# Block 6 of a Strassen GEGLU kernel: another order of its pairs, and other places for a normalization and two weight sums

## The chip, the cores and the metric

The kernel runs on 1 core of one Trainium2 chip. The metric is device time in microseconds (us). The kernel before takes 296.37 us, the median of 3 runs (296.33 to 296.41). TensorE (PE) multiplies, VectorE (DVE), ScalarE (ACT) and GpSimd (POOL) do the rest, and SyncE (SP) issues most DMAs.

## What is computed

An efficient attention (softmax of q over the head's dimension, softmax of k over the sequence, then q times the small matrix k^T v) feeds a gated feed-forward block:

```python
q_s = softmax(q, axis=-1); k_s = softmax(k, axis=2)
kv = np.einsum('bhsd,bhse->bhde', k_s, v)
attn = np.einsum('bhsd,bhde->bhse', q_s, kv)          # 8 batches, 8 heads, 576 x 64
x = attn.transpose(0, 2, 1, 3).reshape(4608, 512)
g = x @ w_gate                                         # 512 x 1536
val = x @ w_val
out = (gelu(g) * val) @ w_out                          # 1536 x 512
```

## The kernel before, in words

The rows of x are worked off in nine blocks of 512: blocks 0 to 7 are the first 512 rows of each batch, and block 8 (B in the code) collects the 64 rows that remain of each of the eight batches. The order is 0 to 6, then 8, then 7. For a block the kernel computes twelve tiles of 128 columns of g and val, applies the gate, keeps the result h as f16 in `ht`, and multiplies it by w_out.

Blocks 0 and 1 compute g and val directly. From block 2 on, much of this is done by a Strassen-Winograd scheme with seven products instead of eight, both for the first multiplication and for the second (`out_strassen`, from block 1 on).

*First multiplication.* Two tiles of columns, k and k + 3, make a pair (`pair_step`, line 662). A pair takes four steps, written "k.i": step 1 does products 1 and 5, step 2 products 6 and 3, step 3 products 7 and 2, step 4 product 4. Each product is four matmuls of 128x256 (`product_gv`, line 626). Between them ACT and DVE carry partial sums: `snap` copies a PSUM tile to SBUF (snq), `add` adds PSUM and snapshot into `cc`, `final` and `upper` apply the gate and write `ht`. The result `cc` of every second pair is kept in the memory of a free buffer (named eq in the profile), the other in a tile of its own. Columns that are not in a pair are done by `half` (line 652): "8g" or "8v" is the gate or value half of tile 8 as four matmuls of 128x512.

The order is a string for each block (lines 641 to 648), worked off by `go_on`. A word "k.i" is a step of a pair, "8g" a half, and any other word calls what the plan holds under that name. FOUR (blocks 2 and 3) has four pairs and four whole tiles, FIVE (blocks 4 and 5) five pairs and two whole tiles (8 and 11), SIX6 (block 6) and SIX (blocks 8 and 7) six pairs. SIX6 knows a step 0, which does product 1 of a pair alone ahead of step 1; its first six steps run at the end of block 5 (lines 860 and 861), before the copy that empties tile psa.

*Sums of the inputs.* The pairs need four differences of parts of x, in `xs`: `sum_x` (line 620) computes them on GpSimd, `sum_x6` (line 613), for block 6 alone, two on GpSimd and two on DVE. They need sums of weights as well: `sum_w1` (line 604) computes those of a late pair, spread over blocks 1 to 5. The sums for pair 8 are needed only by blocks that do pair 8.

*Second multiplication.* `out_strassen` (line 770) does seven products of 12 matmuls each into the PSUM tiles psa, psb and psc, in the order 1, 2, 5, 6, 3, 7, 4 (in blocks 2 to 5 product 7 stands ahead of the last two matmuls of product 3). DVE or ACT takes snapshots (`sn`), and DVE adds them into `yo`, which is stored. The sums of h that products 5, 6 and 3 need are made by `sum_h` (line 576, tiles sh, s and ht) on DVE and GpSimd. The last step of the last pair lies within product 1: in blocks 2 to 5 after three of the six parts of it (`four`, line 804), else after four.

*Other work.* A plan, `at(b, kind, i, functions)`, hangs work on points of a block, and `ride` calls it there: PR points are the words of the order string and a few names, NS points lie within the second multiplication (NS 1 behind the snapshot of psc, NS 2 behind the second snapshot of psa). So the softmax of batch n + 1 is spread over block n: in blocks 2 to 6 its normalizing sums are words "a" and "n" (`norm_pair`, line 233, a reduction of 1280 columns each on DVE), its multiplications words "a", "m" and "p" on GpSimd, and its transposing DMA word "t". `norm_rem0` (line 272) normalizes 64 left-over rows of q of batch 0: a reduction and a reciprocal on DVE, a multiplication on GpSimd, at word "u0" of block 5. Its result goes into a transposing DMA in block 6.

The program is written out in order by hand: every engine runs its instructions in the order in which the code issues them, and a wait holds up all that stands behind it on that engine. PSUM has eight banks, handed out in turn by `big` and `let_go`.

Of the kernel before, what the change touches and what calls it, by code (L numbers as in the profile page):

```python
# [12 lines left out]
ALU = mybir.AluOpType  # L13
# [5 lines left out]
def kernel(  # L19
# [10 lines left out]
    nc = tc.nc  # L30

    B, H, S, D = q.shape
# [4 lines left out]
    NFI = F // P  # L37
# [11 lines left out]
    NO = NFI // 2  # L49
# [43 lines left out]
    def let_go(t):  # L93
        ring.append(held.pop(id(t))[1])
# [19 lines left out]
    xs = const.tile([P, 4, 2, 256], f16)  # L114
# [290 lines left out]
    def get_xt(b):  # L405
        if (b, "xt") not in st:
            st[(b, "xt")] = att.tile([P, HP, MAIN], f16, name="xt", tag="xt")
        return st[(b, "xt")]
# [201 lines left out]
                       3: (a21, a11, a21, ALU.subtract), 4: (t[2], a12, t[1], ALU.subtract)}[i]  # L610
        (nc.gpsimd if eng == "pool" else nc.vector).tensor_tensor(out=o, in0=a, in1=b, op=op)

    def sum_x6():
        xt = get_x(6)
        b11, b12, b21, b22 = (xt[:, c:c + 2, r:r + 256] for c in (0, 2) for r in (0, 256))
        for eng, o, a, b in ((nc.gpsimd, 0, b12, b11), (nc.vector, 1, b22, xs[:, 0]), (nc.vector, 2, b22, b12),
                             (nc.gpsimd, 3, b21, xs[:, 1])):
            eng.tensor_tensor(out=xs[:, o], in0=a, in1=b, op=ALU.subtract)

    def sum_x(xt, xs=xs):  # L620
        b11, b12, b21, b22 = (xt[:, c:c + 2, r:r + 256] for c in (0, 2) for r in (0, 256))
        t = [xs[:, i] for i in range(4)]
        for o, a, b in ((t[0], b12, b11), (t[1], b22, t[0]), (t[2], b22, b12), (t[3], b21, t[1])):
            nc.gpsimd.tensor_tensor(out=o, in0=a, in1=b, op=ALU.subtract)

    def product_gv(i, ps, xt, k, first):
        lo, hi = slice(k * P, (k + 1) * P), slice((k + NO // 2) * P, (k + NO // 2 + 1) * P)
        xs = xs_b[xt is st.get((B - 1, "xt"))]
        for t, w, nm in ((0, wv_sb, "v"), (1, wg_sb, "g")):
# [11 lines left out]
    FOUR = ("a 7g l 7v n 0.1 6.1 0.2 6.2 0.3 6.3 m p 10g 0.4 6.4 1.1 t 10v 1.2 8g 1.3 s0 8v u0 1.4 2.1"  # L641
            " 11g 2.2 11v 2.3 s1")
    FIVE = ("a 8g l 8v n m 0.1 6.1 0.2 6.2 0.3 6.3 0.4 1.1 p 6.4 7.1 t 1.2 7.2 1.3 s0 7.3 2.1 1.4 u0 11g 2.2"
            " y 7.4 11v 2.3 s1")
    SIX6 = ("0.0 6.0 0.1 6.1 a 0.2 6.2 n 0.3 6.3 m 0.4 1.1 6.4 p 7.1 t 1.2 7.2 1.3 s0 7.3 u0 1.4 2.1 7.4 8.1 2.2"
            " 8.2 2.3 8.3 s1 2.4")
    SIX = ("0.1 6.1 0.2 6.2 0.3 6.3 0.4 1.1 6.4 7.1 s0 1.2 7.2 1.3 u0 7.3 1.4 2.1 7.4 8.1 2.2"
           " 8.2 2.3 s1 8.3 2.4")
    steps = {b: (SIX if b >= B - 1 else SIX6 if b == 6 else FIVE if b > 3 else FOUR).split() for b in range(2, B + 1)}
    live, begun = {}, {}  # L650

    def half(b, xt, c, nm):
        t = big([P, 512], f32, "ps" + nm)
# [8 lines left out]
    def pair_step(b, xt, k, i):  # L662
        def final(ps, fi):
            gl = ffn.tile([P, 256], f32, name="glq", tag="gl")
            nc.scalar.activation(out=gl, in_=ps[:, 1], func=ACTF.Gelu)  # L665
            nc.vector.scalar_tensor_tensor(out=ht[:, fi, 0:256], in0=ps[:, 0], scalar=_H_SCALE,  # L666
                                           in1=gl, op0=ALU.mult, op1=ALU.mult)
            let_go(ps)

        def snap(ps, dve=False):  # L670
            sn = ffn.tile([P, 2, 256], f32, name="snq", tag="snq")
            if dve:
                nc.vector.tensor_scalar(out=sn, in0=ps, scalar1=_H_SCALE, scalar2=None, op0=ALU.mult)
            else:
                nc.scalar.activation(out=sn, in_=ps, func=ACTF.Copy, scale=_H_SCALE)  # L675
            return sn

        def add(o, ps, sn):
            nc.vector.scalar_tensor_tensor(out=o, in0=ps, scalar=_H_SCALE, in1=sn,  # L679
                                           op0=ALU.mult, op1=ALU.add)  # L680

        def upper(cc):
            nc.scalar.activation(out=cc[:, :, 1], in_=cc[:, :, 1], func=ACTF.Gelu,  # L683
                                 scale=1.0 / _H_SCALE)
            (nc.vector if k == NFI - NO // 2 - 1 else nc.gpsimd).tensor_tensor(  # L685
                out=ht[:, k:k + NO // 2 + 1:NO // 2, 256:512], in0=cc[:, :, 0], in1=cc[:, :, 1],
                op=ALU.mult)

        if i == 1 and k in begun:
            cc, pa, pb = begun.pop(k)  # L690
        elif i < 2:
            live["odd"] = odd = not live.get("odd", True)
            cc = cc_b[b > 2] if odd else ffn.tile([P, 2, 2, 256], f32, name="cc", tag="cc", bufs=1)
            pa = big([P, 2, 256], f32, "pga", True)
            product_gv(1, pa, xt, k, True)
            pb = big([P, 2, 256], f32, "pgb", True, True)
            nc.scalar.copy(out=pb, in_=pa)  # L697
            if i == 0:
                begun[k] = (cc, pa, pb)
                return  # L700
        if i == 1:
            pc = big([P, 2, 256], f32, "pgc", True)
            product_gv(5, pc, xt, k, True)
            live[k] = [cc, pa, pb, pc, snap(pc, b >= B - 1 or b > 3 and k % NO == 1)]
            return
        cc, pa, pb, pc, s5 = live[k]
        if i == 2:
            product_gv(6, pa, xt, k, False)
            s2 = snap(pa)
            product_gv(3, pc, xt, k, False)  # L710
            add(cc[:, 0], pc, s2)
            let_go(pc)
        elif i == 3:
            product_gv(7, pa, xt, k, False)
            add(cc[:, 1], pa, s5)
            product_gv(2, pb, xt, k, False)
            final(pb, k)
            if k == NFI - NO // 2 - 1 or 3 < b < B - 1 and (k < 2 or k == NO or b == 6):
                live["late"] = lambda: upper(cc)
            elif 3 < b < B - 1 and k == NO + 1:  # L720
                live["y"] = lambda: upper(cc)
            else:
                upper(cc)
        else:
            product_gv(4, pa, xt, k, False)
            if steps[b] and steps[b][0].endswith(".1"):
                live["late"] = lambda: final(pa, k + NO // 2)
            else:
                final(pa, k + NO // 2)

    def go_on(b, xt, upto=None):
        while steps[b] and upto != 0:
            x = steps[b].pop(0)
            late = live.pop("late", None) if "." in x else None
            if "." in x:
                k, i = x.split(".")
                pair_step(b, xt, int(k), int(i))
                upto = upto - 1 if upto else None
            elif x[-1] in "gv" and x[:-1].isdigit():
                half(b, xt, int(x[:-1]), x[-1])  # L740
            elif x == "y":
                live.pop("y")()
            else:
                ride(b, PR, x)
            if late:
                late()
# [17 lines left out]
    def get_x(b):  # L764
        return get_xt(b) if b < B else xtr
# [4 lines left out]
    def out_strassen(b, last):  # L770
        yo = [yop.tile([P, 2, C], f32, name="yo", tag="yo") for _ in range(2)]
        c = (slice(0, 256), slice(256, 512))
# [28 lines left out]

        js = (0, 1, 2, 3, 4, 5) if b < 2 else (0, 3, 1, 4, 2, 5)
        get("a")
        four = 1 < b < B - 2
        cut = 3 if four else 4
        product(1, ps["a"], True, js=js[:cut])
        if four:
# [2 lines left out]
        ride(b, NS, 0)  # L810
        if b < 4:
            ride(b, PR, "u1")
        if b >= B - 2:
            pair_step(b, get_x(b), NFI - NO // 2 - 1, 4)
        get("b")
        product(1, ps["a"], False, js=js[4:])
        if b > 1:
            s1 = snap("a", True)
# [5 lines left out]
        if b < 2:  # L824
            s1 = snap("a")
# [31 lines left out]
        if b == B:  # L857
            go_on(B - 1, get_x(B - 1), 1)
        product(4, ps["a"], False, js=js)
        if b == 5:  # L860
            go_on(6, get_x(6), 6)
        nc.scalar.activation(out=yo[1][:, :, c[0]], in_=tiles_["a"][0], func=ACTF.Copy,
                             scale=1.0 / _H_SCALE)
        let_go(tiles_["a"][0])
# [98 lines left out]
    FI, NS, PR = range(3)  # L963
    plan = {}

    def at(b, kind, i, *fns):
        plan.setdefault((b, kind, i), []).extend(fns)

    L = lambda f, *a: (lambda: f(*a))
# [39 lines left out]
    for b in range(2, B):  # L1009
        n = b + 1  # L1010
# [9 lines left out]
            at(b, PR, "e", L(exp, "q", n + 1), L(exp, "k", n + 1))  # L1020
    at(4, PR, "l", load_rem0)
    at(4, PR, "e", exp_rem0)
    at(5, PR, "u0", norm_rem0)
    at(6, PR, "t", L(unit_trem, 0))
    for b in range(2, B - 1):
        n = b + 1
        at(b, NS, 4, L(unit_x4, n, ("act", "dve"), 0 if n == B - 1 else None))
        at(b, NS, 0, L(unit_kv4, n, True))
        if b < 6:
            at(b, NS, 4, L(preload, ACTF.Gelu))  # L1030
        at(b, NS, 4, sum_x6 if n == 6 else L(lambda n: sum_x(get_x(n)), n if n < B - 1 else B))
    at(B, NS, 2, L(lambda: sum_x(get_x(B - 1), xs_b[1])))
    for b in range(2, B + 1):
        for j in range(NO // 2 - 1):
# [9 lines left out]
                    at(b, PR, "u0", L(sum_h, j, NO, (2,)), L(sum_h, j, NO, (4,), "pool"))  # L1044
    for b, kind, i, dk, x in ((1, FI, 6, 0, 1), (1, FI, 6, 0, 2), (1, FI, 6, 0, 4), (1, FI, 9, 0, 3),
                              (2, NS, 2, 1, 1), (2, NS, 2, 1, 2), (3, NS, 2, 1, 4), (3, NS, 2, 1, 3),
                              (4, NS, 2, 2, 1), (4, NS, 2, 2, 2), (5, NS, 2, 2, 4), (5, NS, 2, 2, 3)):
        at(b, kind, i, L(sum_w1, x, NO + dk, "pool" if b < 2 else "dve"))


    def ride(b, kind, i):
        for fn in plan.get((b, kind, i), []):
            fn()

    for b in order:
        xt = get_xt(b) if b < B else xtr
# [60 lines left out]
```

## Time and profile before

| what | us |
|---|---|
| median of 3 runs | 296.37 |
| the profiled execution | 296.37 |
| its span, first to last instruction | 294.6 |
| PE busy | 282.2 (96%) |
| DVE busy | 231.7 (79%) |
| ACT busy | 199.4 (68%) |
| GpSimd busy | 193.6 (66%) |

The mean granted clock of TensorE is 0.998. 1.77 us of the profiled execution lie outside the span. PE is busy almost throughout, but not quite: the chain of work that ended last is by 87% on PE, by 5% on DVE and by 2% each on GpSimd and ACT.

```profile
PE 87%; DVE 5%; POOL 2%; ACT 2%; issue 2%; ACTq 1%; POOLq 0%
```

In such a chain a share of DVE or GpSimd is a stretch in which PE was held up by that engine. A row of the timeline reads: start, duration, engine, line, operation, output and inputs with shapes, number of instructions merged, and in brackets the idle time of the engine before it and what ended that. Durations of matmuls overlap: the distance of their starts is what they cost.

### The profile page before, as it was taken

The numbers are of one execution on the slowest core, as the hardware profiler recorded it, in microseconds if no ns is written. First come the engines' busy times: TensorE is split into PE (matmuls) and PEld (weight loads), VectorE is DVE, ScalarE is ACT, GpSimd is POOL, SyncE is SP. The second block draws the span as 40 slices with busy tenths as digits, with TensorE's granted clock in tenths as the row PEclk, the third lists the DMA queues.
The fourth block names the chain that finished last, engine by engine and source line by source line (L and its number), as shares of the span: only waits on it lengthen the run. The fifth ranks groups of instructions, "written<-read, shape, count | busy, mean of one in ns | idle before, by whom it ended". The sixth has DMA issues, their size and how long they took to land.

```text
span 294.6 us, 6525 instructions
## 1 busy us (share of the span) xinstructions
PE 282.2 (96%) x2509; PEld 208.4 (71%) x2509; DVE 231.7 (79%) x435; ACT 199.4 (68%) x336; POOL 193.6 (66%) x178
## 2 busy tenths in 40 slices
PE   3999999999999999999999999989799999999994
PEld 1544445446777787778787878777687888888883
DVE  2955889868996789678988898888969579938992
ACT  3763367776687589768967896769675477537650
POOL 1557747995487679857986789766782466293640
PEclk9999999999999999999999999999999999999999
DMA  6999999998069605980598049901150110033003
GB/s 219 373 382 389 401 391 391 333 334 232 3 214 381 121 2 183 384 149 2 163 375 196 2 153 371 193 2 71 73 98 2 75 72 2 1 72 73 2 0 144
DMA packets 54623, 51.73 MB, mean 176 GB/s; under 512 B 18496, under 2 KB 50496, under 8 KB 54592
## 3 DMA queue, kind: packets, MB, share of 16 engines
q1 hardware_dynamic: 52864, 49.49, 53.5%
q10 hardware_dynamic: 1728, 1.84, 1.9%
q8 instruction: 19, 0.31, 0.4%
q14 instruction: 12, 0.10, 0.1%
HBM read 37.75 MB, written 9.44 MB: 160 GB/s over the span
## 4 chain that ended last, share of the span: by engine, by line
PE 87%; DVE 5%; POOL 2%; ACT 2%; issue 2%; ACTq 1%; POOLq 0%
PE pga L636 19%; PE psa L760 13%; PE psg L471 10%; PE psv L471 10%; PE pgc L636 10%; PE psc L760 7%; PE pgb L636 4%; PE psb L760 4%; PE psy L539 4%; PE pswarm L463 2%; PE pskv L347 1%; POOL ht L685 1%; DVE yo L798 1%; ACT L466 1%; POOL s L586 1%
## 5 line engine op out<-in xcount | busy, mean ns | idle before, releaser
L636 PEld LDWEIGHTS <-wgv_sb 128*128 128x128 f16 x576 | 55.7, 98 | 12.9 <-DVE cc L679 1.8
L471 PEld LDWEIGHTS <-wgv_sb 128*128 128x128 f16 x288 | 27.9, 98 | 29.1 <-issue 0.7
L760 PEld LDWEIGHTS <-ht 128*128 128x128 f16 x384 | 36.5, 98 | 9.2 <-issue 2.5
L248 POOL TENSOR_TENSOR eq<-eq,rrq 128x640 f16<-128x640 f16 (+1 forms) x27 | 34.8, 1304 | 12.1 <-DVE rrq L240 8.8
L685 POOL TENSOR_TENSOR ht<-cc 128x512 f16<-128x512 f32 x18 | 23.2, 1288 | 25.3 <-ACT cc L683 25.3
L471 PE MATMUL psg<-xt,wgv_sb 128*128 128x512 f16 x144 | 39.0, 379 | 0.0
L471 PE MATMUL psv<-xt,wgv_sb 128*128 128x512 f16 x144 | 38.9, 379 | 0.0
L636 PE MATMUL pga<-xs,wgv_sb 128*128 128x256 f16 x240 | 35.7, 273 | 1.9 <-DVE cc L679 1.5
L586 POOL TENSOR_TENSOR s<-ht,sh 128x512 f16<-128x512 f16 x14 | 16.2, 1155 | 18.3 <-DVE sh L586 18.3
L665 ACT ACTIVATE glq<-pgb 128x256 f32<-128x256 f32 x36 | 13.7, 380 | 20.6 <-PE pgb L636 14.6
L476 ACT ACTIVATE gl<-psg 128x512 f32<-128x512 f32 x24 | 13.8, 597 | 16.6 <-PE psg L471 15.4
L186 POOL CAST v<-vt 128x640 f16<-128x640 f32 x26 | 19.8, 803 | 7.7 <-PE pskv L347 6.2
L697 ACT COPY pgb<-pga 128x512 f32<-128x512 f32 x36 | 20.9, 582 | 5.7 <-PE pga L636 5.3
L666 DVE SCALAR_TENSOR_TENSOR ht<-pga,glq 128x256 f16<-128x256 f32 x36 | 15.0, 420 | 12.0 <-ACT glq L665 11.6
L477 DVE SCALAR_TENSOR_TENSOR ht<-psv,gl 128x512 f16<-128x512 f32 x24 | 16.0, 686 | 10.1 <-PE psv L471 8.4
L675 ACT ACTIVATE snq<-pga 128x512 f32<-128x512 f32 x36 | 21.4, 600 | 3.7 <-PE pga L636 3.2
L760 PE MATMUL psa<-tw,ht 128*128 128x256 f16 x192 | 23.4, 272 | 0.2 <-DVE yo L798 0.2
L586 POOL TENSOR_TENSOR ht<-ht 128x512 f16<-128x512 f16 x16 | 18.8, 1179 | 7.2 <-DVE sh L586 7.2
L210 ACT ACTIVATE ek<-kt 128x1280 f16<-128x1280 f32 (+1 forms) x11 | 19.1, 1748 | 5.9 <-DMA kt<-in_k_dram 4.2
L685 POOL TENSOR_TENSOR ht<-eq 128x512 f16<-128x512 f32 x15 | 19.1, 1274 | 4.2 <-ACT eq L683 4.2
L238 DVE TENSOR_REDUCE rq<-eq 128x20 f32<-128x1280 f16 (+1 forms) x12 | 17.2, 1432 | 4.5 <-ACT eq L210 4.5
L760 PEld LDWEIGHTS <-sh 128*128 128x128 f16 x192 | 18.7, 98 | 2.5 <-DVE sn L792 0.3
(178 smaller groups left out, 687.8 us busy)
## 6 DMA issues: line engine op xcount, KB each, us to landing
out_dram<-yo SPq DMA_DIRECT2D x15, 512.0 KB, 3.1
kt<-in_k_dram SPq DMA_DIRECT2D x7, 640.0 KB, 8.6
vt<-in_v_dram SPq DMA_DIRECT2D x7, 640.0 KB, 5.2
qt<-in_q_dram SPq DMA_DIRECT2D x7, 640.0 KB, 7.1
qt<-in_q_dram SPq DMA_DIRECT2D x8, 512.0 KB, 7.6
wost<-in_moe_w_out_dram SPq DMA_DIRECT2D x6, 512.0 KB, 7.9
kt<-in_k_dram SPq DMA_DIRECT2D x6, 512.0 KB, 9.8
vt<-in_v_dram SPq DMA_DIRECT2D x6, 512.0 KB, 5.7
```

The lines of the kernel that those rows point to most:

```text
L186: nc.gpsimd.tensor_copy(out=dst, in_=src)
L210: nc.scalar.activation(out=dst[:, n0:NC, h0 * D:h1 * D].rearrange(o, d=D, **({"t": 2} if b >= QUAD else {})), in_=heads(tiles[(nm, b)], b, ...
L238: nc.vector.reduce_sum(rq, e, axis=mybir.AxisListType.X)
L248: (nc.gpsimd if eng == "pool" else nc.vector).tensor_tensor(out=e, in0=e, in1=rrq.unsqueeze(-1).to_broadcast((P, n, 2, D)), op=ALU.mult)
L471: nc.tensor.matmul(ps, w[:, ci, fi * P:(fi + 1) * P], xt[:, ci, :], start=(ci == 0), stop=(ci == HP - 1))
L477: nc.vector.scalar_tensor_tensor(out=ht[:, fi, :], in0=psv, scalar=_H_SCALE, in1=gl, op0=ALU.mult, op1=ALU.mult)
L586: (nc.gpsimd if eng == "pool" else nc.vector).tensor_tensor(out=o, in0=a, in1=b, op=op)
L636: nc.tensor.matmul(ps[:, t], a, x, start=(first and t == 0 and c == 0), stop=(c == 1), skip_group_check=True)
L675: nc.scalar.activation(out=sn, in_=ps, func=ACTF.Copy, scale=_H_SCALE)
L685: (nc.vector if k == NFI - NO // 2 - 1 else nc.gpsimd).tensor_tensor(out=ht[:, k:k + NO // 2 + 1:NO // 2, 256:512], in0=cc[:, :, 0], in1=c ...
L697: nc.scalar.copy(out=pb, in_=pa)
L760: nc.tensor.matmul(ps[t], a, w, start=(first and j == js[0] and (t == ts[0] or ps[t].tensor is not ps[ts[0]].tensor)), stop=(j == js[-1]), ...
```

## The change

Block 6 does FIVE instead of SIX6: five pairs and the whole tiles 8 and 11, with nothing of it ahead of the end of block 5. SIX6, step 0 and `sum_x6` go; the differences of x for block 6 are made by `sum_x`, four on GpSimd. The conditions in `out_strassen` and `pair_step` that named block 6 follow. `norm_rem0` moves from word "u0" to NS 1 of block 5. The last two weight sums for pair 8 move from NS 2 of block 5 to NS 1 and NS 2 of block 6.

```diff
-    def sum_x6():
-        xt = get_x(6)
-        b11, b12, b21, b22 = (xt[:, c:c + 2, r:r + 256] for c in (0, 2) for r in (0, 256))
-        for eng, o, a, b in ((nc.gpsimd, 0, b12, b11), (nc.vector, 1, b22, xs[:, 0]), (nc.vector, 2, b22, b12),
-                             (nc.gpsimd, 3, b21, xs[:, 1])):
-            eng.tensor_tensor(out=xs[:, o], in0=a, in1=b, op=ALU.subtract)
...
     FIVE = ("a 8g l 8v n m 0.1 6.1 0.2 6.2 0.3 6.3 0.4 1.1 p 6.4 7.1 t 1.2 7.2 1.3 s0 7.3 2.1 1.4 u0 11g 2.2"
             " y 7.4 11v 2.3 s1")
-    SIX6 = ("0.0 6.0 0.1 6.1 a 0.2 6.2 n 0.3 6.3 m 0.4 1.1 6.4 p 7.1 t 1.2 7.2 1.3 s0 7.3 u0 1.4 2.1 7.4 8.1 2.2"
-            " 8.2 2.3 8.3 s1 2.4")
...
-    steps = {b: (SIX if b >= B - 1 else SIX6 if b == 6 else FIVE if b > 3 else FOUR).split() for b in range(2, B + 1)}
-    live, begun = {}, {}
+    steps = {b: (SIX if b >= B - 1 else FIVE if b > 3 else FOUR).split() for b in range(2, B + 1)}
+    live = {}
...
-        if i == 1 and k in begun:
-            cc, pa, pb = begun.pop(k)
-        elif i < 2:
+        if i == 1:
...
-            if i == 0:
-                begun[k] = (cc, pa, pb)
-                return
-        if i == 1:
...
-            if k == NFI - NO // 2 - 1 or 3 < b < B - 1 and (k < 2 or k == NO or b == 6):
+            if k == NFI - NO // 2 - 1 or 3 < b < B - 1 and k < 2 or 3 < b < B - 1 and k == NO:
                 live["late"] = lambda: upper(cc)
...
-        four = 1 < b < B - 2
+        four = 1 < b < B - 1
...
-        if b >= B - 2:
+        if b >= B - 1:
             pair_step(b, get_x(b), NFI - NO // 2 - 1, 4)
...
-        if b == 5:
-            go_on(6, get_x(6), 6)
...
-    at(5, PR, "u0", norm_rem0)
+    at(5, NS, 1, norm_rem0)
...
-        at(b, NS, 4, sum_x6 if n == 6 else L(lambda n: sum_x(get_x(n)), n if n < B - 1 else B))
+        at(b, NS, 4, L(lambda n: sum_x(get_x(n)), n if n < B - 1 else B))
...
-                              (4, NS, 2, 2, 1), (4, NS, 2, 2, 2), (5, NS, 2, 2, 4), (5, NS, 2, 2, 3)):
+                              (4, NS, 2, 2, 1), (4, NS, 2, 2, 2), (6, NS, 1, 2, 4), (6, NS, 2, 2, 3)):
```

## The prediction

> **What bounds the kernel now.** I read the list of engines first: TensorE (PE) is busy for 282.2 of 294.6 us, so a change counts when it gives PE less work or lets it wait less. The list of PE's waits comes second, since it says how much waiting there is and for whom:
>
> ```profile
> PE pswarm L463 <- ACT warm L909: 4.9, 1, 4.9
> PE pga L636 <- DVE cc L679: 1.5, 1, 1.5
> PE psa L760 <- DVE ht L666: 1.1, 1, 1.1
> PE pgc L636 <- ACT snq L675: 0.3, 1, 0.3
> ```
>
> The first line is the start of the program, and the change leaves it alone. The next two are single waits on VectorE (DVE). To place them I cut the span at the starts of the second output product (tile psb) of blocks 3, 4, 5, 6 and 8, the order in which they run, and asked for the stretches. The columns are the window, its length, then busy time of PE, weight loads, DVE, ACT and GpSimd (POOL), each with its instructions, the granted clock, and DMA:
>
> ```profile
> 133.32:162.94 29.62, 29.62 (x298) 24.12 (x296) 25.61 (x48) 23.74 (x40) 24.37 (x23) 1.00 0.60 183
> 162.94:194.02 31.08, 29.87 (x298) 24.04 (x296) 26.73 (x51) 24.17 (x42) 24.40 (x23) 1.00 0.58 170
> 194.02:226.36 32.34, 30.19 (x310) 25.15 (x308) 27.39 (x51) 25.35 (x44) 21.37 (x19) 1.00 0.20 56
> 226.36:255.11 28.75, 28.72 (x278) 24.70 (x276) 23.00 (x48) 18.26 (x40) 15.36 (x13) 1.00 0.10 38
> ```
>
> The reader is to see that the first two rows hold the same 298 matmuls (block 4 and block 5 run in the same order, FIVE), and that the second is 1.46 us longer. The third (block 6, in the order SIX6) is 2.72 us longer than the first. The clock is full in all of them. So I need the timeline at two places. First the end of block 5, on PE, DVE and POOL:
>
> ```profile
> 193.79 0.39 PE L760 MATMUL psa<-wo_sb,ht 128*128 128x256 f16 x2 [1.08 <-DVE ht L666]
> ...
> 187.46 0.67 DVE L275 TENSOR_REDUCE rq<-eq0r 64x8 f32<-64x512 f16 x1
> 188.16 0.20 DVE L277 RECIPROCAL rrq<-rq 64x8 f32<-64x8 f32 x1
> ...
> 191.93 1.48 DVE L586 TENSOR_TENSOR sh<-ht 128x512 f16<-128x512 f16 x1 [0.82 <-POOL ht L685]
> 193.33 0.41 DVE L666 SCALAR_TENSOR_TENSOR ht<-pga,glq 128x256 f16<-128x256 f32 x1
> ...
> 188.44 1.11 POOL L278 TENSOR_TENSOR eq0r<-eq0r,rrq 64x512 f16<-64x512 f16 x1 [0.60 <-DVE rrq L277]
> ```
>
> L275 to L278 are norm_rem0. Its GpSimd multiplication stands ahead of GpSimd's product of upper halves (L685); the sum on DVE (L586) waits 0.82 us for that product and then takes 1.48 us, where the same sum took 0.42 us in block 4 (at 161.26); the final product of the last pair (L666) stands behind that sum, and PE waits 1.08 us for it. Then the start of block 6:
>
> ```profile
> 210.01 0.61 PE L636 MATMUL pga<-xs,wgv_sb 128*128 128x256 f16 x4 [1.48 <-DVE cc L679]
> ...
> 206.27 0.69 DVE L679 SCALAR_TENSOR_TENSOR cc<-pgc,snq 128x512 f32<-128x512 f32 x1 [0.28 <-ACT snq L675]
> 207.01 0.69 DVE L679 SCALAR_TENSOR_TENSOR eq<-pgc,snq 128x512 f32<-128x512 f32 x1
> 207.62 1.48 DVE L238 TENSOR_REDUCE rq<-eq 128x20 f32<-128x1280 f16 x1
> 209.13 0.28 DVE L240 RECIPROCAL rrq<-rq 128x20 f32<-128x20 f32 x1
> 209.33 0.63 DVE L679 SCALAR_TENSOR_TENSOR cc<-pga,snq 128x512 f32<-128x512 f32 x1
> ```
>
> In SIX6 the pairs come at once, so the second normalizing reduction of batch 7 (1.48 + 0.28 us) lies between additions that free PE's banks, and PE waits 1.48 us. In block 5 the two reductions stand at 172.08 and 174.58, beside PE's two whole halves (171.53 to 173.29) and the first products; PE has no wait there.
>
> **The change, part by part.**
>
> *norm_rem0 leaves "u0" of block 5.* After it block 5 has, up to its psb, the instructions of block 4 in the order of block 4, only with the buffers eq and cc exchanged. So 31.08 becomes 29.62: minus 1.46 us. Bounds: 1.08 us (the wait itself) to 1.46.
>
> *It goes behind the snapshot of psc in block 5.* Taken by block 4's times (subtract 31.08 from block 5's), DVE starts that snapshot at 165.76 and is free for the next at 166.36; there norm_rem0 starts, 0.67 and 0.20 us, until about 167.18. The snapshot of psa, at 167.08 until now, moves to 167.18 and ends at 167.87; PE takes up psa again (product 7) at 167.97. So the cover is product 3 on psc, and 0.1 us of it is left. I take 0.05 us; at worst the reduction waits out GpSimd's sum (166.12 to 167.28) and the snapshot is 0.95 us late, so 0.85. On POOL the multiplication (1.11 us) lands at 167.28, ahead of four casts of v (3.10): they end at 171.4 in place of 170.3. The first difference of x started at 171.48, waiting for ACT's copy of xt, so it is not late; PE takes the result at 173.72, it is there at 172.63. Cost 0, and 0 to 0.1 if ACT's copy comes early. SP's queue gets nothing there: the transposing DMA of eq0r stays in block 6.
>
> *Block 6 goes from SIX6 to FIVE.* Work: four 128x256 matmuls take 0.437 us of PE, four 128x512 take 0.865 (starts in block 5). A pair is 28 of the small ones, 3.06 us; the four halves that replace the sixth pair are 16 large ones, 3.46 us: plus 0.40 us. Order: the six steps that ran during the end of block 5 are gone, and PE has 1.73 us of halves ahead of the first pair, as in blocks 4 and 5. Block 6 then has block 5's PE order, the same allocation order of PSUM banks, and on DVE, ACT and POOL the same sequence, without the two exponentials of the remainder (0.40 us each on ACT) and without weight sums ahead of it. So I price the whole stretch by the undisturbed row: 32.34 becomes 29.62, minus 2.72 us; that is 3.12 us of waiting gone, 0.40 more work. Bounds: the two waits that are listed for it are 1.48 + 0.30, so at least 1.78 - 0.40 = 1.38; at most 2.72.
>
> *sum_x6 becomes four subtractions on GpSimd.* Four times 1.15 us (L624) instead of two there and two on DVE (0.43, 0.42). DVE gains 0.85 us ahead of its reductions. In block 5 the third and fourth results stood at 174.98 and 176.08 and were wanted at 176.78 and 178.53; it ran just so without a wait. Cost 0; it is inside the 29.62.
>
> *The last weight sums move from block 5 to the end of block 6.* They took 0.49 and 0.93 us (L611). In block 6 DVE has them between the addition of psb (ends 229.83) and that of psc, for which it waited 2.21 us; 1.42 fits. No queue but DVE's gets them. Their first reader is pair 8 of block 8 (248.95), almost 20 us later. Cost 0; where both wait out GpSimd's two sums there (1.16 each, 229.31 to 231.58) they end near 232.4, the psc addition (232.04) slips by 0.4, and the addition of psa behind it, which PE's product 4 needs, by 0.3.
>
> The Trainium skill ("SBUF — State Buffer", section "SBUF: two separate sides") says that VectorE and GpSimd share one port pair, that an operation of VectorE with two SBUF inputs and one of GpSimd exclude each other for the whole instruction. The 1.48 us row agrees with it, and the rule speaks against the new place of the weight sums and against four subtractions on GpSimd; by the rule the sum below would be 0.3 us worse, 292.4. It would not stop a reduction, which has one input, and L238 keeps its 1.47 us beside the subtractions of block 5.
>
> *The stretch behind block 6.* PE's third product started 0.17 us late (227.84, after psb at 226.36 and 1.31 us of work) because DVE's sums were late; in block 4 it wasn't. Minus 0.17, bounds 0 and 0.17. Blocks 8 and 7 keep their order; only two buffers change places.
>
> **The sum.** 294.60 - 1.46 + 0.05 - 2.72 - 0.17 = 290.30 us of span. The profiled run took 296.37, which is also the median, so 1.77 us lie around the span: 292.07, say 292.1.
>
> **The rivals.**
>
> A wait in FIVE at block 6 takes the place of the old one. For it: DVE has no reserve there; in block 5 the addition that PE's step at 178.53 needs ends at 178.47. Against: all that feeds it is as early as in block 5 or earlier. If norm_rem0's 1.11 us on GpSimd pass through in the way they did in block 5, 1.1 to 1.5 us come back: 293.2 to 293.6.
>
> The psa snapshot is held up by the whole GpSimd sum: 0.85 us, 292.9.
>
> Nothing is won, because block 6 is late for reasons that both orders share (DVE is busy 27.39 us in it): only block 5's 1.46 is gone and the 0.40 of work is added, or the snapshot eats the first as well: 295.3 to 296.4. Against it stands the row of block 4, with 25.61 us of DVE and no wait.
>
> Slower: GpSimd shuts VectorE out at the start of block 6. With four subtractions (4.6 us) and the multiplication (1.11) in front, DVE could lose up to 5.7 us before its first additions, and PE there has no reserve. That would be 292.1 + 5.7 = 297.8; it ends above the old time by more than 0.2% once 4.9 us of the 5.7 are lost. Against it: the same four in block 5 left DVE's reductions at 1.47 and 1.48 us.
>
> **How the numbers follow.** Both gains as worked out: 0.78, with its own range 291.6 to 292.7. Snapshot held up: 0.05. A new wait in block 6: 0.09. Nothing or little won: 0.04. Slower: 0.04. The likeliest gives 292.1. Its upside is nearly used up: 291.5 would take all bounds and the 0.40 of work hidden in remaining gaps. The range 291.5 to 293.6 takes in the first three cases. 0.2% is 0.6 us, about what a measurement of this kernel can tell from no change: faster 0.93, same 0.03, slower 0.04.
>
> **What would show it.** Right: cut at psb, the stretches of blocks 5 and 6 both last 29.6 to 29.8 us; no PE wait on ht L666 at the end of block 5 nor on cc L679 in block 6; the sum on DVE in block 5 back at 0.42 us. Wrong: PE waits at psa for sn (L792) in block 5, for xs or a cc addition in block 6, or an addition of yo that starts late behind L611 at the end of block 6.

## The result, and the profile after

The changed kernel takes 292.15 us (median of 4 runs, 292.11 to 292.29) against 296.39 for the kernel before in the runs beside it (296.33 to 296.54): a ratio of 0.9857, 95% interval 0.984 to 0.9874, so 1.4% faster. The forecast was 292.1. Its span is 290.3 us, 4.3 less than before.

The list of PE's waits of the changed kernel has one line left, the one at the start of the program:

```profile
PE pswarm L463 <- ACT warm L892: 4.9, 1, 4.9
```

The stretches between the starts of psb, in the changed kernel, columns as before (blocks 4, 5, 6, then 8):

```profile
133.40:163.02 29.62, 29.62 (x298) 24.11 (x296) 25.63 (x48) 23.74 (x40) 24.35 (x23) 1.00 0.62 183
163.02:192.65 29.63, 29.63 (x298) 24.11 (x296) 25.49 (x49) 24.16 (x42) 23.28 (x22) 1.00 0.60 179
192.65:222.28 29.63, 29.63 (x299) 24.12 (x297) 24.75 (x49) 23.73 (x40) 23.93 (x23) 1.00 0.22 61
222.28:250.85 28.57, 28.53 (x278) 24.80 (x276) 24.33 (x47) 18.18 (x39) 15.60 (x14) 1.00 0.10 39
```

Before, the last three were 31.08, 32.34 and 28.75. The differences, 1.45, 2.71 and 0.18 us, are the 4.3 us of the span. In all three rows PE is now busy for the whole stretch, within 0.04 us.

The timeline of the changed kernel at the two new places, the end of block 5 and the end of block 6 (line numbers have moved: L777, L783 and L745 were L792, L798 and L760):

```profile
195.47 0.69 DVE L777 TENSOR_SCALAR sn<-psc 128x512 f32<-128x512 f32 x1 [0.24 <-PE psc L745]
196.08 0.67 DVE L275 TENSOR_REDUCE rq<-eq0r 64x8 f32<-64x512 f16 x1
196.78 0.19 DVE L277 RECIPROCAL rrq<-rq 64x8 f32<-64x8 f32 x1
196.90 0.63 DVE L777 TENSOR_SCALAR sn<-psa 128x512 f32<-128x512 f32 x1
...
197.06 1.03 POOL L278 TENSOR_TENSOR eq0r<-eq0r,rrq 64x512 f16<-64x512 f16 x1
198.04 2.70 POOL L186 CAST v<-vt 128x640 f16<-128x640 f32 x4
...
224.78 1.00 DVE L611 TENSOR_TENSOR kt<-wgv_sb,kt 128x512 f16<-128x512 f16 x1
225.70 1.37 DVE L611 TENSOR_TENSOR wgv_sb<-wgv_sb 128x512 f16<-128x512 f16 x1
227.79 0.69 DVE L783 SCALAR_TENSOR_TENSOR yo<-psc,sn 128x512 f32<-128x512 f32 x1 [0.72 <-PE psc L745]
```

The snapshot of psa ends at 197.53 and PE takes psa up at 197.68. The two weight sums take 2.3 us in block 6, not 1.42, and end at 227.07; the addition behind them still waits 0.72 us for PE.

### The profile page after: what moved, and what is told of

Its sections match the earlier page's. It is cut to its first block, busy times and chain, and to the rows that moved or that the text cites. A ratio compares the mean times of both kernels' runs of the same rounds, so it can differ in the third digit from the quotient of the medians.

```text
span 290.3 us, 6495 instructions
## 1 busy us (share of the span) xinstructions
PE 281.3 (97%) x2497; PEld 207.4 (71%) x2497; DVE 229.4 (79%) x430; ACT 197.8 (68%) x332; POOL 195.1 (67%) x180
## 4 chain that ended last, share of the span: by engine, by line
PE 95%; DVE 2%; ACTq 1%; ACT 1%; issue 0%
PE pga L629 21%; PE psa L745 14%; PE psg L471 11%; PE psv L471 11%; PE pgc L629 11%; PE psc L745 7%; PE pgb L629 5%; PE psb L745 4%; PE psy L539 4%; PE pswarm L463 2%; PE pskv L347 1%; PE psx L434 1%; ACTq L166 1%; DVE yo L783 1%; PE pst L372 1%; PE psx L413 1%
## 5 line engine op out<-in xcount | busy, mean ns | idle before, releaser
L745 PEld LDWEIGHTS <-ht 128*128 128x128 f16 x384 | 36.6, 98 | 7.4 <-issue 2.5
L471 PE MATMUL psg<-xt,wgv_sb 128*128 128x512 f16 x152 | 41.1, 379 | 0.0
L471 PE MATMUL psv<-xt,wgv_sb 128*128 128x512 f16 x152 | 41.0, 379 | 0.0
L676 POOL TENSOR_TENSOR ht<-eq 128x512 f16<-128x512 f32 x17 | 21.6, 1272 | 19.7 <-ACT eq L674 19.6
L629 PE MATMUL pga<-xs,wgv_sb 128*128 128x256 f16 x232 | 34.5, 273 | 0.0
L676 POOL TENSOR_TENSOR ht<-cc 128x512 f16<-128x512 f32 x16 | 20.4, 1275 | 7.1 <-ACT cc L674 7.1
L657 DVE SCALAR_TENSOR_TENSOR ht<-pga,glq 128x256 f16<-128x256 f32 x35 | 14.8, 422 | 12.0 <-ACT glq L656 11.8
L745 PE MATMUL psa<-tw,ht 128*128 128x256 f16 x192 | 23.4, 272 | 0.2
L745 PEld LDWEIGHTS <-sh 128*128 128x128 f16 x192 | 18.7, 98 | 2.5 <-DVE sn L777 0.3
```

The lines of the kernel that those rows point to most:

```text
L471: nc.tensor.matmul(ps, w[:, ci, fi * P:(fi + 1) * P], xt[:, ci, :], start=(ci == 0), stop=(ci == HP - 1))
L629: nc.tensor.matmul(ps[:, t], a, x, start=(first and t == 0 and c == 0), stop=(c == 1), skip_group_check=True)
L745: nc.tensor.matmul(ps[t], a, w, start=(first and j == js[0] and (t == ts[0] or ps[t].tensor is not ps[ts[0]].tensor)), stop=(j == js[-1]), ...
```

## Experiments

**norm_rem0 moved, block 6 left in SIX6**

```diff
--- kernel before
-    at(5, PR, "u0", norm_rem0)
+    at(5, NS, 1, norm_rem0)
```

> The kernel before with one edit: norm_rem0 hangs at NS 1 of block 5 and not at word u0; block 6 keeps SIX6. Theory: block 5's lost time (1.46 us) is norm_rem0's alone, so 296.4 - 1.46 + 0.05 = 295.0, the stretch from psb of block 4 to psb of block 5 falls to 29.6, and block 6 stays at 32.3. Rival: block 6, which can't start earlier than its inputs, eats the gain; then 296.0 to 296.4, with block 6's stretch growing to 33 or more.

Measured: 296.51 us, a ratio to the kernel before of 1.0016, 95% interval 0.9997 to 1.0034: no gain. The stretch of block 5 does fall, 163.13 to 192.76, 29.63 us. But the gain is lost at the end of block 5's second multiplication, in a place that the rival did not name. DVE, GpSimd and PE in the timeline of this kernel:

```profile
197.01 0.63 DVE L792 TENSOR_SCALAR sn<-psa 128x512 f32<-128x512 f32 x1
197.57 2.90 DVE L611 TENSOR_TENSOR kt<-wgv_sb,kt 128x512 f16<-128x512 f16 x1
200.40 0.93 DVE L611 TENSOR_TENSOR wgv_sb<-wgv_sb 128x512 f16<-128x512 f16 x1
201.26 0.68 DVE L798 SCALAR_TENSOR_TENSOR yo<-psa,sn 128x512 f32<-128x512 f32 x1
...
197.17 1.04 POOL L278 TENSOR_TENSOR eq0r<-eq0r,rrq 64x512 f16<-64x512 f16 x1
198.16 2.90 POOL L186 CAST v<-vt 128x640 f16<-128x640 f32 x4
...
201.99 2.72 PE L760 MATMUL psa<-tw,ht 128*128 128x256 f16 x12 [1.89 <-DVE yo L798]
```

The first weight sum, 0.49 us before, takes 2.90. It is still in block 5 here, and stands behind norm_rem0. The addition to yo is late by that, and PE's product 4 waits 1.89 us for it. So norm_rem0's new place is free only because the change also takes the weight sums out of it. (Seven of the ten runs lie at 296.3 to 296.7, three at 298.1 to 298.3, and the timeline is of one of these; the clock behind the wait makes the difference, see the last section.)

**norm_rem0 back at "u0"**

```diff
--- changed kernel
-    at(5, NS, 1, norm_rem0)
+    at(5, PR, "u0", norm_rem0)
```

> The changed kernel with norm_rem0 back at word u0 of block 5; block 6 in FIVE. Theory: the two gains add, so 292.15 + 1.4 = 293.6, with PE's wait for ht L657 back at about 1.1 us. Rival: block 6 in FIVE has reserves and takes up the delay, 292.2 to 292.6.

Measured: 293.66 us, 1.51 more than the changed kernel. The wait is back in PE's list:

```profile
PE psa L745 <- DVE ht L657: 1.1, 1, 1.1
```

Block 5 takes 31.10 us and block 6 stays at 29.63: FIVE takes up nothing of the delay. The theory holds.

**norm_rem0 cut in two**

```diff
--- changed kernel
+    at(5, PR, "u0", norm_rem0)      # reduction and reciprocal, VectorE
-    at(5, NS, 1, norm_rem0)
+    at(5, NS, 1, mul_rem0)          # multiplication, GpSimd
```

> The changed kernel with norm_rem0 cut in two: reduction and reciprocal (0.87 us, VectorE) at word u0 of block 5, the multiplication (1.11 us, GpSimd) at NS 1. Theory: GpSimd's multiplication ahead of its product of upper halves made the wait in block 5; VectorE's part alone costs 0 to 0.4, so 292.2 to 292.6. Rival: VectorE's 0.87 us pass straight through to PE, 293.0 to 293.6, as much as the whole of norm_rem0 costs there.

Measured: 292.41 us. Of the 1.51 us that norm_rem0 costs at "u0", VectorE's 0.87 us of work make 0.26, and GpSimd's multiplication, added to it there, the other 1.25. The theory holds.

**One reduction of batch 7 left out in SIX6**

```diff
--- kernel before, norm_rem0 moved
-            at(b, PR, "n", L(norm_pair, n, 1, 0, ()))
+            at(b, PR, "n", L(norm_reuse, n) if n == 7 else L(norm_pair, n, 1, 0, ()))
```

> e1 (kernel before, norm_rem0 moved) and in block 6 the second normalizing reduction and reciprocal of batch 7 (1.48 + 0.28 us on VectorE) are left out; the second half of the heads is normalized with the first half's factors, so part of the softmax of q of batch 7 is not computed. SIX6 stays. Theory: PE's 1.48 us wait in block 6 is this reduction between two additions; it goes, and the time is e1's less 1.5 to 1.7, about 293.3; what is left of block 6's loss (some 1.4 us) has other causes. Rival: SIX6's early steps take PSUM banks and ACT's time, whatever VectorE does; then the wait only changes place and the time stays within 0.4 us of e1's 295.0.

Measured: 295.81 us as a median of ten runs. Five of them, with a mean granted clock of 0.997 or more, lie at 294.9 to 295.2, and five, with 0.993 to 0.994, at 296.5 to 296.8 (see the last section). The first five compare with the seven runs at 296.3 to 296.7 of the kernel that it was made from: 1.5 us less. In its list of PE's waits (L804 is the addition to yo) there is no cc any more; its first line, the start of the program, is left out here:

```profile
...
PE psa L766 <- DVE yo L804: 2.0, 2, 1.9
PE psx L428 <- DVE kv_sb L336: 0.2, 1, 0.2
PE pga L642 <- ACT snq L681: 0.2, 1, 0.2
```

The wait behind the weight sum stays. The theory's difference holds; its absolute 293.3 does not, because it did not know of that wait.

**The reductions among the pairs, with five pairs**

```diff
--- changed kernel, block 6 alone
-    FIVE = ("a 8g l 8v n m 0.1 6.1 0.2 6.2 0.3 6.3 0.4 1.1 p ...
+    FIVE6 = ("8g 8v 0.1 6.1 a 0.2 6.2 n 0.3 6.3 m 0.4 1.1 p ...
```

> The changed kernel, where in block 6 alone the normalizing words stand among the pairs as in SIX6 (8g 8v 0.1 6.1 a 0.2 6.2 n 0.3 6.3 m), five pairs and the whole tiles as in FIVE. Theory: what cost 1.48 us in SIX6 is the place of the reductions between the additions, not the sixth pair or the early steps; the wait for a cc addition comes back with 1.0 to 1.7 us, 293.2 to 293.9. Rival: it was the sixth pair's load on VectorE; with five pairs the same place costs 0 to 0.3, 292.15 to 292.5.

Measured: 294.03 us. The wait is back with the size that it had in SIX6 (1.50 us, there 1.48), in PE's list:

```profile
PE pga L629 <- DVE cc L672: 1.5, 1, 1.5
```

Block 6 takes 31.27 us, 1.64 more. Five pairs or six, it is the place of the reductions that makes this wait. The 1.64 us are about half of the 3.12 us of waiting that the prediction counted in SIX6; the other half does not come back here.

**A third reduction in FIVE**

```diff
--- changed kernel, word "n" of block 6
+        norm_pair(b, 1, 0, ())
         norm_pair(b, 1, 0, ())
```

> The changed kernel with the second normalizing reduction and reciprocal of batch 7 done twice in a row in block 6 (1.48 + 0.28 us more on VectorE at the same word, to a second buffer). Theory: in FIVE the first additions are just in time (in block 5 the one that PE needs at 178.53 ended at 178.47), with 0.4 us of idle time ahead of them, so of 1.76 us about 1.3 come through at once: 293.4 to 293.6, as a wait for cc L679's successor. Rival: FIVE's two whole halves at the front cover the reductions with room to spare, 292.2 to 292.5.

Measured: 294.61 us, 2.46 more, beyond both ranges. Block 6 grows by 1.88 (192.41 to 223.92), with a PE wait of 1.73 us for the cc addition; some 0.75 lie behind the last matmul (last section). The edit put more on VectorE than its 1.76 us of work. The last of the three reciprocals, in this kernel, and the first addition of the changed kernel:

```profile
207.81 0.28 DVE L240 RECIPROCAL rrq<-rq 128x20 f32<-128x20 f32 x1 [0.85 <-POOL eq L248]
...
206.30 0.69 DVE L670 SCALAR_TENSOR_TENSOR cc<-pgc,snq 128x512 f32<-128x512 f32 x1 [0.44 <-ACT snq L666]
```

The tile rrq has two buffers (`bufs=2`, line 239), so the third reciprocal waits 0.85 us until GpSimd's multiplications have read the first. Between the end of the second reciprocal and the first addition lie 2.40 us, where the changed kernel has 0.44. The addition is 1.95 us later by that, and 1.88 come through to PE. So the reserve of 0.4 us in the expectation was right, and the work that it was set against was too small.

**Two "free" parts undone at once, then each alone**

```diff
--- changed kernel
-        at(b, NS, 4, L(lambda n: sum_x(get_x(n)), n if n < B - 1 else B))
+        at(b, NS, 4, sum_x6 if n == 6 else L(lambda n: sum_x(get_x(n)), n if n < B - 1 else B))
...
-     ... (6, NS, 1, 2, 4), (6, NS, 2, 2, 3)):
+     ... (5, NS, 2, 2, 4), (5, NS, 2, 2, 3)):
```

> The changed kernel with two of its four parts undone: the differences of x for block 6 split between GpSimd and VectorE again (sum_x6), and the last two weight sums of pair 8 back at NS 2 of block 5. Theory: both were costed at nothing, so 292.15 within 0.2. Rival: VectorE has no reserve at the start of block 6; 0.85 us of differences, or 1.42 us of sums, pass through to PE, 293.0 to 293.6.

Measured: 295.10 us, 2.95 more: the theory falls, and the rival's range is passed too. In this kernel block 6 reads weights of tile 11 that the second sum has already overwritten, so it computes something else for that tile; the work is the same. This is a second reason why the sums have to move with the order. The weight sum takes 2.90 us here as well, and PE waits 1.88 us for the addition to yo; some 0.75 us more lie behind the last matmul (last section). Taken apart:

```diff
--- changed kernel: only the first weight sum back
-     ... (6, NS, 1, 2, 4), (6, NS, 2, 2, 3)):
+     ... (5, NS, 2, 2, 4), (6, NS, 2, 2, 3)):
```

> The changed kernel with only the first of the two moved weight sums (0.49 us where it stood before) back at NS 2 of block 5, behind norm_rem0. New theory, from the weight sum that took 2.90 us when norm_rem0 alone was moved: VectorE's sum with two SBUF inputs is kept out while GpSimd runs the multiplication of norm_rem0 and the casts of v without a gap, so it takes 2.5 to 2.9 us again, the addition of psa behind it starts near 200.3 instead of 199.2, PE's product 4 waits 0.9 to 1.1 us: 293.0 to 293.3. Rival: the long wait belongs to the pair of sums and to SIX6's early steps; one sum fits into VectorE's 1.65 us of idle time, 292.15 to 292.4.

Measured: 293.34 us, just above the theory's range; PE waits 1.0 us for the addition of psa, which starts at 200.27. And with GpSimd's multiplication out of the way:

```diff
--- the same, and
-    at(6, PR, "t", L(unit_trem, 0))
+    at(6, PR, "t", mul_rem0, L(unit_trem, 0))
```

> The kernel of the run with one sum back, and GpSimd's multiplication of norm_rem0 (1.04 us) moved to word t of block 6, where GpSimd idles 1.96 us; reduction and reciprocal stay at NS 1 of block 5. Theory: without the multiplication ahead of the casts, the weight sum meets GpSimd as in the kernel before and takes 0.5 to 0.9 us; no wait of PE, 292.15 to 292.4. Rival: the casts alone shut VectorE out, since its sum now comes some 0.1 to 0.2 us later than in the kernel before; 293.0 or more.

Measured: 292.10 us (292.01 to 292.15), the same as the changed kernel. The two timelines at the weight sum, first with the multiplication ahead of the casts:

```profile
197.44 2.91 DVE L611 TENSOR_TENSOR kt<-wgv_sb,kt 128x512 f16<-128x512 f16 x1
...
197.04 1.04 POOL L278 TENSOR_TENSOR eq0r<-eq0r,rrq 64x512 f16<-64x512 f16 x1
198.03 2.90 POOL L186 CAST v<-vt 128x640 f16<-128x640 f32 x4
```

then without it (L615 is the same sum):

```profile
197.38 0.47 DVE L615 TENSOR_TENSOR kt<-wgv_sb,kt 128x512 f16<-128x512 f16 x1
...
196.86 2.91 POOL L186 CAST v<-vt 128x640 f16<-128x640 f32 x4
```

The sum starts at the same time in both. It takes 0.47 us where GpSimd is within its first cast, and 2.91 where GpSimd is within the multiplication. The size and the place of the wait are as the theory had them in both runs. But GpSimd's four casts follow one another without a gap in both, so it is not enough that GpSimd leaves no gap, as the theory had it: what differs is the operation that the sum met.

The differences of x alone:

```diff
--- changed kernel: only
-        at(b, NS, 4, L(lambda n: sum_x(get_x(n)), n if n < B - 1 else B))
+        at(b, NS, 4, sum_x6 if n == 6 else L(lambda n: sum_x(get_x(n)), n if n < B - 1 else B))
```

> The changed kernel with only the differences of x for block 6 split between GpSimd and VectorE again (sum_x6). Theory: they are free in both places, 292.15 within 0.2, no wait of PE. Rival: 0.85 us more on VectorE ahead of the two reductions pass through to the first additions, which are just in time: 292.7 to 293.0.

Measured: 293.31 us, 1.16 more. Block 6 takes 30.05 us (192.50 to 222.55), 0.42 more; the other 0.75 or so is again behind the last matmul. PE's list has the wait for the addition:

```profile
PE pga L636 <- DVE cc L677: 0.3, 1, 0.3
```

So the rival's mechanism holds, with half of the 0.85 us that VectorE has to do: the idle 0.44 us ahead of the first addition take up the other half. Its range, 292.7 to 293.0, does not hold: without the 0.75 us at the end the time would be 292.6.

**Six pairs, with VectorE relieved**

```diff
--- kernel before, norm_rem0 at NS 1 of block 5, the last two weight sums taken out of the plan, and for n == 7
+                at(5, NS, 2, L(norm_pair, n, 0, 0, ()))
+                at(b, PR, "a", L(norm_mul, n, 0, "pool"), L(norm_mul, n, 1, "pool"), L(norm_pair, n, 1, 0, ()),
+                   L(sum_w1, 4, NO + 2, "pool"), L(sum_w1, 3, NO + 2, "pool"))
```

> The kernel before in SIX6, norm_rem0 at NS 1 of block 5, and VectorE relieved in block 6: batch 7's first reduction at NS 2 of block 5 (where VectorE idles 1.65 us), the second at word a ahead of the first addition, GpSimd's multiplications from word a on, and the last two weight sums on GpSimd behind the first two multiplications. Nothing is left out. Theory: with no reduction between the additions the 1.48 us wait goes, and of block 6's 3.1 us of waits 1.0 to 1.5 stay (ACT's table load, late sums of h), against 0.40 less work of PE than FIVE: 292.6 to 293.3. Rival: six pairs need more of VectorE than there is, 294 to 295; or all waits go, and the sixth pair's 0.40 makes it 291.8.

Measured: 293.59 us, a little above the range. Block 6 takes 31.18 us. PE's list has these waits left:

```profile
PE pga L636 <- DVE cc L679: 0.4, 1, 0.4
PE pgc L636 <- ACT snq L675: 0.3, 1, 0.3
PE pga L636 <- ACT snq L675: 0.2, 1, 0.2
```

0.9 us are listed; against 29.63 less 0.40 of work, 1.95 us are lost. The list shows less because it counts a gap from the modelled end of a matmul: its wait of 0.3 us for snq moves PE's next start by 0.47, and gaps of some 0.3 us by starts are listed as 0.2 or not at all. To this, the table of Gelu later (e6 is the kernel just described):

```diff
--- the same, and
-            at(b, NS, 4, L(preload, ACTF.Gelu))
+            at(*((6, PR, "n") if b == 5 else (b, NS, 4)), L(preload, ACTF.Gelu))
```

> e6 with ACT's load of the Gelu table (1.28 us) moved from the end of block 5 to word n of block 6, behind the first copies and snapshots. Theory: PE's wait of 0.3 to 0.5 us for snq at the start of block 6 goes: 0.3 to 0.5 less than e6. Rival: the load then lies ahead of the first Gelu, which holds a PSUM bank, and the time is the same or up to 0.6 longer than e6.

Measured: 293.69 us, 0.10 more than e6: no gain, as the rival had it. No version of six pairs that was tried reaches the changed kernel.

## Why the prediction was right

*Block 5, minus 1.46.* Measured 1.45, by the row of block 4. The runs with norm_rem0 back (plus 1.51) and cut in two (plus 0.26) show that it was the cause, and for the most by its GpSimd part. The sum on VectorE at the end of block 5 is back at 0.42 us (at 190.97), as the prediction asked.

*Block 6, 32.34 to 29.62.* Measured 29.63. Pricing the stretch by an undisturbed row of the same order carried it, not a sum of single waits. The reason given, a reduction between two additions, is shown twice: taken out of SIX6 it gives 1.5 us, put into FIVE it costs 1.64. That is about half of the 3.12 us of waiting that the row held. The other half did not come back with the reductions in FIVE, and SIX6 without a reduction there still lost 1.95 us (the first of the two runs with VectorE relieved). So it seems to go with six pairs or with their early steps; which of the two was not tried, and the prediction did not need it, since the row of FIVE has neither.

*norm_rem0 in its new place, 0.05.* Nothing is lost between psb of block 5 and that of block 6. The snapshot came as worked out, within 0.1 us; the casts took 2.70 us and not 3.10. But the step looked only at what stands behind norm_rem0 in the changed kernel. The edits were costed one by one, and they are not independent: with the weight sums left where they were, the same move loses all it gained. The sum came out because the change moves both.

*Weight sums, cost 0.* Right for their new place: they took 2.3 us, 0.9 more than the rows of before, with room for 0.7 more. Missed is what their leaving is worth once norm_rem0 stands ahead of them: one of them at the old place costs 1.2 us, and both make PE wait 1.9. With GpSimd's multiplication out of the way, one of them there costs nothing (292.10).

*Four subtractions on GpSimd, cost 0.* Here the prediction's own words, that VectorE gains 0.85 us ahead of its reductions, were worth 0.42 us in block 6. It was contained in the row of block 4, so the sum was not off; as a term of its own it was sized at 0.

*The stretch behind block 6, minus 0.17.* Measured 0.18.

*The rivals.* None came. The wait that takes the place of the old one had its condition named nearly rightly: the reserve ahead of the first additions is not nothing but 0.44 us, as the third reduction and the split differences show. The rule of the Trainium skill ("SBUF — State Buffer", section "SBUF: two separate sides") that was weighed against the change fits the longer sums (1.00 and 1.37 us beside GpSimd's two), but they had room: they start 2.50 us behind psb, where the prediction, going by SIX6's late row, had 3.47. So 292.1 by the row stood against 292.4 by the rule.

## What to carry to other kernels

Where a stretch runs again in an order that another stretch already has without waits, price it by that whole row; it holds what single terms miss. Cost the edits of one change together as well: a move can be free only because another edit empties the place that it goes to. When VectorE has little reserve (here 0.44 us), look for small operations that stand between a result and the engine that waits for it, and ask what GpSimd runs beside them.

## What the runs showed of the hardware

*VectorE kept out by GpSimd.* A sum of two SBUF tensors on VectorE (128x512, f16) took 0.47 to 0.49 us where it met the first of GpSimd's four casts (the kernel before, and the one with the multiplication later), and 2.90 to 2.91 us where it met GpSimd's multiplication with the four casts behind it. The Trainium skill ("SBUF — State Buffer", section "SBUF: two separate sides") says that such a sum and a GpSimd operation that reads SBUF exclude each other for a whole instruction. The runs show more: VectorE's one instruction waited through several of GpSimd's in a row, the multiplication's rest and three of the casts. In the kernel with one sum back the first three casts took 0.71 to 0.72 us each and the fourth, within which the sum ends, 0.91. What decides who comes next was not tried.

*The clock.* In the kernel with norm_rem0 moved, three of ten runs were some 1.8 us longer, and in the one with a reduction left out as well, five of ten by 1.6. The profiled run of the first kernel is one of its three; windows of its timeline, columns as above, the first up to the end of the wait and the second behind it:

```profile
192.76:201.99 9.23, 7.34 (x79) 6.08 (x77) 8.96 (x15) 8.71 (x8) 7.16 (x9) 1.00 0.01 2
201.99:205.00 3.01, 3.01 (x15) 2.09 (x15) 2.90 (x7) 0.51 (x2) 0.82 (x2) 0.50 0.41 166
```

After a wait of 1.89 us the granted clock was 0.50 in the window of 3 us behind it. It stays there until 205.43 and is 1.00 from then on; 3.4 us at half the clock cost 1.7 us of work, so the wait cost almost twice its length. In the kernel with both sums back the same wait (1.88 us) left the clock at full in all runs. The Trainium skill ("TensorE: Matmul & The Clock Gate", "Part 1: The HAM clock gate (the "warmup" mystery)") names an idle window of about 3.4 us, free-running, as the condition; here 1.89 us was enough in some runs, so the measurement decides.

*Behind the last matmul.* Three kernels (both sums back, third reduction, differences split) end some 0.75 us later after the start of their last psb than all others (12.6 us behind it against 11.8). They are those with 432 recorded VectorE instructions. The traces show one more difference. Each of these three has a fetch of code on instruction queue q14 that starts 10.0 us after the last psb: 2.0 us behind the last matmul, while the last stores are being written. The last data packet of the stores ends at 11.0 us after psb there, and at 10.3 in all other kernels. In the kernels with 433 to 435 VectorE instructions the last such fetch starts at 6.8 to 7.0 us, under PE's last products; in those with 430 none falls between 280 us and the end of the span. So the fetch fits the lost time in place and in all fourteen traces, but no run moved it alone, and the cause stays open.
